# Re-ordering the first batch's chain of an attention-and-MLP kernel: halves of G, pair 1's scores first, and a q wrap read by split matmuls

## The chip, the cores and the metric

The kernel runs on one core of one Trainium2 chip. The metric is the device time of one execution in microseconds, as a median of several executions. The span in a profile is about 1.8 us shorter than that time. Each execution also records the mean clock that was granted to TensorE over the span, 1.0 being full speed.

## The reference

A small attention with 8 batches, 8 heads, 512 local and 32 global positions and head size 64 feeds a two-layer MLP with a hard-swish gate. Local queries see a band of 32 positions each way and all global keys.

```python
k_all = np.concatenate([k_g, k_l], axis=2)
v_all = np.concatenate([v_g, v_l], axis=2)
out_g = np.matmul(sm(scale * np.matmul(q_g, k_all.transpose(0, 1, 3, 2))), v_all)
mask = np.abs(pos[:, None] - pos[None, :]) <= 32
s_ll = np.where(mask, scale * np.matmul(q_l, k_l.transpose(0, 1, 3, 2)), -1e9)
s_l = np.concatenate([scale * np.matmul(q_l, k_g.transpose(0, 1, 3, 2)), s_ll], axis=-1)
out_l = np.matmul(sm(s_l), v_all)
# ... heads side by side -> x of 4352 rows by 512
h = x @ w_in
out = (h * np.clip(h + 3.0, 0.0, 6.0) / 6.0) @ w_out
```

## The kernel before

Two heads of a batch form a "pair", so a batch has four pairs. For batches 0 and 1 TensorE transposes k and q. "G" is the transposed k_g. It is broadcast into free columns of kT (`kglob`), v_g likewise into the shifted V (`vglob`). The scores of a pair come in two chunks: chunk 0 needs only the pair's own k, chunk 1 also needs G. The q of a pair is stored with its last 32 columns repeated in front (the "wrap"), so that every score matmul reads 128 consecutive columns. In batch 0, VectorE copies that wrap out of the q that ScalarE has just written.

```python
def emit_T(p, qdve=False):              # cut: transposes of k and q into PSUM
    nc.vector.tensor_copy(out=kv[...], in_=ps["k"])             # k copy
    qcopy(out=qT[:, W:Sl + W], in_=ps["q"])                     # q copy, ScalarE or VectorE
    if b == 0:
        nc.vector.tensor_copy(out=qT[:, 0:W], in_=qT[:, Sl:Sl + W])   # the wrap
    ...

# opening (cut), every engine in program order
warm_up(17)            # filler matmuls on zeros
...
emit_T(0); emit_Sm(0, 0); emit_Sm(0, 1); emit_Ss(0, 0)   # masks, then pair 0's chunk 0
warm_up(3)
emit_T(1)
emit_G(0, 1, "kg"); kglob(0, nc.vector); vglob(0, nc.vector)
emit_Ss(0, 1)          # pair 0's chunk 1: needs G
emit_S(1, 0)           # pair 1's chunk 0: does not
emit_T(2); emit_S(1, 1); warm_up(2); emit_S(2, 0)
...
```

The softmax here doesn't subtract the row's maximum and nothing guards it: scores larger than these inputs give would overflow.

## Time and profile before

| | before |
|---|---|
| first timed runs | 319.76, 321.0, 321.62, 322.47 us |
| the profiled execution | 319.11 us, span 317.3, clock 0.999 |
| TensorE busy | 305.0 us, 96% of the span |
| TensorE idle from 5 to 50 us | 6.4 us |

The lines that carried the reading are in the prediction below: the page's head, busy time by stretches, what TensorE waits for, and the chain of waits around pair 1.

### The profile page before, as it was taken

To read this page: it belongs to the slowest core of one execution; us is meant where nothing else is said; L and a number is where in the kernel's file an instruction comes from. 1 tells how busy PE (TensorE), PEld (TensorE's weight loads), DVE (VectorE), ACT (ScalarE), POOL (GpSimd) and SP (SyncE) were. 2 spreads that over 40 slices of the span, in tenths; PEclk is the share of its full clock that TensorE was granted. 3 is DMA by queue.
4 is the path that set the end of the run, shared out by engine and by line. 5 is a ranking of instruction groups with operands and counts; after the bars stand their busy time and mean duration, and the time that the engine had idled before them with its cause. 6 is when DMAs were issued, how large, how long until landed. Compare 5 with 4: busy or idle time off the path is not lost.

```text
span 317.3 us, 7316 instructions
## 1 busy us (share of the span) xinstructions
PE 305.0 (96%) x2674; PEld 162.7 (51%) x2674; DVE 214.5 (68%) x486; ACT 199.7 (63%) x416; POOL 152.8 (48%) x273
## 2 busy tenths in 40 slices
PE   8698899999999999999999999999999999999995
PEld 5454564545555455555555555555555554448444
DVE  5578688897755898679955886468934962379101
ACT  6647777887443995479844994589656941589000
POOL 4777998598866654763675456444410000000000
PEclk9999999999999999999999999999999999999999
DMA  7999999999999998799999996999542002100131
GB/s 207 258 301 333 298 310 314 219 192 216 204 222 231 173 204 144 162 202 203 163 156 209 204 188 138 164 213 160 112 115 86 17 19 83 66 2 1 35 99 66
DMA packets 140260, 53.05 MB, mean 167 GB/s; under 512 B 127552, under 2 KB 131904, under 8 KB 140224
## 3 DMA queue, kind: packets, MB, share of 16 engines
q1 hardware_dynamic: 138048, 52.32, 76.2%
q0 software_dynamic: 2176, 0.26, 1.3%
q8 instruction: 21, 0.34, 0.5%
q14 instruction: 15, 0.12, 0.2%
HBM read 35.13 MB, written 8.91 MB: 139 GB/s over the span
## 4 chain that ended last, share of the span: by engine, by line
PE 79%; DVE 12%; ACT 3%; issue 2%; DMA 2%; SPq 0%; POOL 0%
PE po L455 35%; PE psH L439 29%; DVE gt L446 5%; PE psS L268 3%; DVE xn L358 2%; DVE E L275 2%; PE pav L350 2%; PE pav L353 2%; DMA stg<-in_q_l_dram 2%; PE psSG L324 1%; PE psS L293 1%; PE po L467 1%; PE pg L390 1%; PE psS L281 1%; PE psX L411 1%
## 5 line engine op out<-in xcount | busy, mean ns | idle before, releaser
L455 PE MATMUL po<-wout,gt 128*128 128x512 f16 x528 | 122.6, 379 | 0.0
L439 PE MATMUL psH<-xt,win 128*128 128x512 f16 x512 | 119.3, 379 | 1.5 <-DVE gt L446 1.4
L446 DVE SCALAR_TENSOR_TENSOR gt<-t,psH 128x512 f16<-128x512 f32 (+1 forms) x144 | 89.9, 651 | 19.6 <-ACT t L444 18.9
L444 ACT ACTIVATE t<-psH,half_col 128x512 f32<-128x512 f32 (+1 forms) x144 | 92.3, 670 | 14.5 <-PE psH L439 12.9
L439 PEld LDWEIGHTS <-win 128*128 128x128 f16 x576 | 53.3, 98 | 52.6 <-issue 1.6
L455 PEld LDWEIGHTS <-gt 128*128 128x128 f16 x528 | 48.4, 98 | 52.2
L275 DVE TENSOR_TENSOR E<-E,mk 128x512 f16<-128x512 f16 x96 | 51.4, 580 | 30.9 <-ACT E L272 30.2
L272 ACT ACTIVATE E<-psS 128x512 f16<-128x512 f32 x96 | 49.8, 604 | 13.7 <-PE psS L268 13.6
L459 ACT COPY ot<-po 128x512 f32<-128x512 f32 x16 | 9.4, 586 | 58.6 <-PE po L455 53.1
L140 POOL CAST kn<-stg 128x512 f16<-128x512 f32 x31 | 19.0, 614 | 31.8 <-DMA stg<-in_k_l_dram 31.1
L376 POOL TENSOR_TENSOR s<-Eg 128x128 f32<-128x128 f16 x24 | 10.8, 450 | 39.5 <-ACT Eg L325 39.0
L459 DVE COPY ot<-po 128x512 f32<-128x512 f32 x17 | 11.7, 689 | 22.9 <-PE po L455 22.3
L358 DVE TENSOR_TENSOR xn<-pav,rc 128x256 f16<-128x256 f32 x64 | 26.0, 421 | 1.3
L140 POOL CAST qn<-stg 128x512 f16<-128x512 f32 x31 | 19.5, 629 | 11.4 <-DMA stg<-in_q_l_dram 10.4
L140 POOL CAST vt<-stg 128x512 f16<-128x512 f32 x32 | 21.1, 659 | 7.2 <-DMA stg<-in_v_l_dram 6.0
L144 POOL COPY vb<-vt 64x512 f16<-64x512 f16 x32 | 21.4, 669 | 2.1
L302 ACT ACTIVATE E<-psS 128x512 f16<-128x512 f32 x32 | 16.9, 607 | 8.1 <-PE psS L293 8.1
L350 PE MATMUL pav<-vt,E 128*128 128x65 f16 x256 | 19.9, 194 | 0.0
L353 PE MATMUL pav<-vb,E 128*128 128x65 f16 x256 | 19.9, 195 | 0.0
L350 PEld LDWEIGHTS <-E 128*128 128x128 f16 x256 | 17.9, 99 | 3.3
L353 PEld LDWEIGHTS <-E 128*128 128x128 f16 x256 | 16.8, 97 | 3.1
L268 PEld LDWEIGHTS <-kT 64*128 64x128 f16 x384 | 10.8, 94 | 9.8 <-issue 7.9
(92 smaller groups left out, 276.6 us busy)
## 6 DMA issues: line engine op xcount, KB each, us to landing
stg<-in_k_l_dram SPq DMA_DIRECT2D x32, 256.0 KB, 3.6
stg<-in_q_l_dram SPq DMA_DIRECT2D x32, 256.0 KB, 4.0
stg<-in_v_l_dram SPq DMA_DIRECT2D x32, 256.0 KB, 4.6
out_dram<-ot SPq DMA_DIRECT2D x23, 256.0 KB, 3.6
stg<-in_moe_w_in_dram SPq DMA_DIRECT2D x16, 256.0 KB, 5.9
stg<-in_moe_w_out_dram SPq DMA_DIRECT2D x16, 256.0 KB, 4.8
out_dram<-ot SPq DMA_DIRECT2D x8, 192.0 KB, 3.6
out_dram<-ot SPq DMA_DIRECT2D x16, 64.0 KB, 1.8
```

The costliest lines, as they stand in the source:

```text
L140: eng.tensor_copy(out=o, in_=s[c + "f"])
L144: eng.tensor_copy(out=vbs[b % NV][0:D, :, m, vc], in_=vts[b % NV][D:P, :, m, vc])
L272: nc.scalar.activation(out=E[:, ch, e], in_=pss[2 * ch + e], func=EXP, scale=qk_scale)
L275: nc.vector.tensor_tensor(out=E[:, ch, e], in0=E[:, ch, e], in1=mk[:, ch].rearrange("p w c -> p (w c)"), op=mult)
L350: nc.tensor.matmul(out=o, lhsT=E[:, 0, e, w * P:(w + 1) * P], rhs=vt[:, w, m, c], start=True, stop=False, skip_group_check=True)
L353: nc.tensor.matmul(out=o, lhsT=E[:, 1, e, w * P:(w + 1) * P], rhs=vb[:, (w - 1) % NT, m, c], start=False, stop=True, skip_group_check=True)
L358: nc.vector.tensor_tensor(out=xn[:, 2 * w2:2 * w2 + 2].rearrange("p w (e d) -> p w e d", e=2), in0=po[:, :, 1:1 + P].rearrange("p w (e d) ...
L439: nc.tensor.matmul(out=ps[:, 0:n], lhsT=w_in_t[m][:, c * P:(c + 1) * P], rhs=rhs(m), start=(m == 0), stop=(m == NM - 1), skip_group_check= ...
L444: nc.scalar.activation(out=t1[:, 0:n], in_=ps[:, 0:n], func=RELU, bias=half_col, scale=1.0 / 6.0)
L446: nc.vector.scalar_tensor_tensor(out=gts[c][:, 0:n], in0=t1[:, 0:n], scalar=1.0, in1=ps[:, 0:n], op0=amin, op1=mult)
L455: nc.tensor.matmul(out=po[t][:, 0:dm], lhsT=gts[c][:, t * P:(t + 1) * P], rhs=w_out_t[c // 4][:, c % 4], start=(c == 0), stop=(c == NC - 1))
L459: (nc.scalar.copy if t % 2 else nc.vector.tensor_copy)(out=ot, in_=po[t][:, 0:dm])
```

## The change

It shortens the chain at the start, where TensorE waits for small copies on VectorE and ScalarE. G's copies and broadcasts go in halves, so that pair 0's second chunk needs only the first half. Pair 1's first chunk goes ahead of pair 0's second one. The wrap is no longer copied in batch 0: the first block of a score row is computed by two matmuls, 32 columns from the end of q and 96 from its start. Pair 4's transposes move behind the broadcast for batch 1, three copies change engine (pair 2's q to VectorE, pair 3's q and pair 2's x to ScalarE), two fillers go, and two loads are moved.

```diff
+            parts = [(w * P, w * P, P)]
+            if w == 0 and p < NM:
+                parts = [(0, Sl, W), (W, W, P - W)]
+            for o, i, n in parts:
+                for e in range(2):
+                    nc.tensor.matmul(out=pss[e][:, o:o + n], lhsT=kT[r, c0:c0 + P], rhs=qT[r, i:i + n], ...)
 ...
+    load_g(1, 4, "kg")
     load(4, "kq")
-    load_g(1, 4, "kg")
 ...
-    load_vg(1)                       # was among the first loads
 ...
     cast(4, "kq", nc.gpsimd)
+    load_vg(1)
 ...
-    emit_T(1)
-    emit_G(0, 1, "kg")
-    kglob(0, nc.vector)
-    vglob(0, nc.vector)
-    emit_Ss(0, 1)
+    emit_Tp(1); copy_k(1); copy_q(1)           # one per line in the kernel
     emit_S(1, 0)
+    emit_Gp(0, 1, "kg")
+    copy_G(0, 1, "kg", 0); kglob_m(0, lo)
+    emit_S(0, 1)
+    copy_G(0, 1, "kg", 1); kglob_m(0, hi)
 ...
-    warm_up(2)
+    vglob_m(0, lo)
 ...
-    emit_T(4)
     cast_G(1, 4, "kg")
 ...
     kglob(1, nc.vector)
+    emit_T(4)
```

More of the change, by code (lines that the diff above doesn't have):

```diff
@@ L192, in cast_G, with emit_Gp @@
         gst[b0, nm, "n"] = n
-    def emit_G(b0, b1, nm):
+    def emit_Gp(b0, b1, nm):
         nb = b1 - b0
@@ L198, in emit_G @@
         n = gst[b0, nm, "n"]
-        psT = ps_tile("psGT", FP16)
+        psT = gst[b0, nm, "ps"] = ps_tile("psGT", FP16)
         for j in range(nb):
@@ L202, in emit_G, with copy_G, kglob_m, vglob_m @@
                              rhs=ident, is_transpose=True)
-        MH = NM // HH
-        for x in range(HH):
-            kv = psT[x * D:(x + 1) * D, 0:nb * P].rearrange("p (b m e s) -> p e b m s", b=nb, m=MH, e=2)
-            for e in range(2):
-                r, ms = slice(e * D, (e + 1) * D), slice(x * MH, (x + 1) * MH)
-                o = kgT[r, ms, b0:b1] if nm == "kg" else qgz[r, ms, b0:b1, e]
-                nc.vector.tensor_copy(out=o.rearrange("p m b s -> p b m s"), in_=kv[:, e])
+    MH = NM // HH
+    def copy_G(b0, b1, nm, x):
+        nb = b1 - b0
+        kv = (gst[b0, nm, "ps"][x * D:(x + 1) * D, 0:nb * P]
+              .rearrange("p (b m e s) -> p e b m s", b=nb, m=MH, e=2))
+        for e in range(2):
+            r, ms = slice(e * D, (e + 1) * D), slice(x * MH, (x + 1) * MH)
+            o = kgT[r, ms, b0:b1] if nm == "kg" else qgz[r, ms, b0:b1, e]
+            nc.vector.tensor_copy(out=o.rearrange("p m b s -> p b m s"), in_=kv[:, e])
+    def emit_G(b0, b1, nm):
+        emit_Gp(b0, b1, nm)
+        for x in range(HH):
+            copy_G(b0, b1, nm, x)
+    def kglob_m(b, ms):
+        kv = kTs[b % 2][:, ms, 0:NT * KW].rearrange("p m (u c) -> p m u c", u=NT)
+        n = ms.stop - ms.start
+        nc.vector.tensor_copy(out=kv[:, :, :, P:KW],
+                              in_=kgT[:, ms, b].unsqueeze(2).to_broadcast([P, n, NT, Sg]))
+    def vglob_m(b, ms):
+        n = ms.stop - ms.start
+        nc.vector.tensor_copy(
+            out=vbs[b % NV][rg, :, ms, vc],
+            in_=vg[rg, b].rearrange("s (m h) d -> s m (h d)", h=2)[:, ms].unsqueeze(1)
+            .to_broadcast([Sg, NT, n, P]))
     def kglob(b, eng):
@@ L214, in kglob, with emit_Tp, copy_k, copy_q @@
                         in_=kgT[:, :, b].unsqueeze(2).to_broadcast([P, NM, NT, Sg]))
-    def emit_T(p, qdve=False):
+    def emit_Tp(p):
         b, m = divmod(p, NM)
         s = st[p]
-        kT = kTs[b % 2][:, m]
-        kv = kT[:, 0:NT * KW].rearrange("p (u c) -> p u c", u=NT)
-        qT = wrk.tile([P, Sl + W], FP16, tag="qT", name="qT", bufs=5)
-        ps = {}
+        s["kT"] = kTs[b % 2][:, m]
+        s["qT"] = wrk.tile([P, Sl + W], FP16, tag="qT", name="qT", bufs=5)
         for c in "kq":
-            ps[c] = ps_tile("psT" + c, FP16)[:, 0:Sl]
+            s["ps" + c] = ps_tile("psT" + c, FP16)[:, 0:Sl]
             for j in range(NT):
-                nc.tensor.matmul(out=ps[c][:, j * P:(j + 1) * P], lhsT=s[c + "n"][:, j], rhs=ident,
-                                 is_transpose=True)
-        qcopy = nc.vector.tensor_copy if qdve else nc.scalar.copy
+                nc.tensor.matmul(out=s["ps" + c][:, j * P:(j + 1) * P], lhsT=s[c + "n"][:, j],
+                                 rhs=ident, is_transpose=True)
+    def copy_k(p):
+        s = st[p]
+        kv = s["kT"][:, 0:NT * KW].rearrange("p (u c) -> p u c", u=NT)
         nc.vector.tensor_copy(
             out=kv[:, :, 0:P].rearrange("p u (i j) -> p u i j", j=NT),
-            in_=ps["k"].rearrange("p (j u i) -> p u i j", j=NT, u=NT))
-        qcopy(out=qT[:, W:Sl + W].rearrange("p (i j) -> p i j", j=NT),
-              in_=ps["q"].rearrange("p (j i) -> p i j", j=NT))
-        if b == 0:
-            nc.vector.tensor_copy(out=qT[:, 0:W], in_=qT[:, Sl:Sl + W])
-        else:
-            nc.scalar.copy(out=qT[:, 0:W].rearrange("p (i j) -> p i j", j=NT),
-                           in_=ps["q"].rearrange("p (j i) -> p i j", j=NT)[:, P - W // NT:P])
-        s["qT"], s["kT"] = qT, kT
+            in_=s["psk"].rearrange("p (j u i) -> p u i j", j=NT, u=NT))
+    def copy_q(p, dve=False):
+        s = st[p]
+        (nc.vector.tensor_copy if dve else nc.scalar.copy)(
+            out=s["qT"][:, W:Sl + W].rearrange("p (i j) -> p i j", j=NT),
+            in_=s["psq"].rearrange("p (j i) -> p i j", j=NT))
+    def emit_T(p):
+        emit_Tp(p)
+        copy_k(p)
+        copy_q(p)
+        s = st[p]
+        nc.scalar.copy(out=s["qT"][:, 0:W].rearrange("p (i j) -> p i j", j=NT),
+                       in_=s["psq"].rearrange("p (j i) -> p i j", j=NT)[:, P - W // NT:P])
     def emit_TD(p):
@@ L290, in emit_Ss @@
             c0 = w * KW if ch == 0 else ((w - 1) % NT) * KW + D
-            for e in range(2):
-                r = slice(e * D, (e + 1) * D)
-                nc.tensor.matmul(out=pss[e][:, w * P:(w + 1) * P], lhsT=kT[r, c0:c0 + P],
-                                 rhs=qT[r, w * P:(w + 1) * P], start=False, stop=True,
-                                 skip_group_check=True)
+            parts = [(w * P, w * P, P)]
+            if w == 0 and p < NM:
+                parts = [(0, Sl, W), (W, W, P - W)]
+            for o, i, n in parts:
+                for e in range(2):
+                    r = slice(e * D, (e + 1) * D)
+                    nc.tensor.matmul(out=pss[e][:, o:o + n], lhsT=kT[r, c0:c0 + P],
+                                     rhs=qT[r, i:i + n], start=False, stop=True,
+                                     skip_group_check=True)
         if exps:
@@ L398, in emit_den, with emit_X @@
                          rhs=Ess[b].rearrange("p m e s -> p (m e s)"), skip_group_check=True)
-    def emit_X(p):
+    def emit_X(p, act=False):
         b, m = divmod(p, NM)
@@ L414, in emit_X @@
         xts.setdefault(b, []).append(xt)
-        nc.vector.tensor_copy(out=xt, in_=psX[:, 0:Sl])
+        (nc.scalar.copy if act else nc.vector.tensor_copy)(out=xt, in_=psX[:, 0:Sl])
     def emit_XG(b):
@@ L619 @@
     u1 = units.pop(0)
-    emit_T(0)
-    emit_Sm(0, 0)
-    emit_Sm(0, 1)
-    emit_Ss(0, 0)
-    warm_up(3)
-    emit_T(1)
-    emit_G(0, 1, "kg")
-    kglob(0, nc.vector)
-    vglob(0, nc.vector)
-    emit_Ss(0, 1)
-    emit_S(1, 0)
-    emit_T(2)
+    lo, hi = slice(0, NM // 2), slice(NM // 2, NM)
+    HEAD = 3
+    emit_Tp(0)
+    copy_k(0)
+    copy_q(0)
+    emit_S(0, 0)
+    warm_up(3)
+    emit_Tp(1)
+    copy_k(1)
+    copy_q(1)
+    emit_S(1, 0)
+    emit_Gp(0, 1, "kg")
+    copy_G(0, 1, "kg", 0)
+    kglob_m(0, lo)
+    emit_S(0, 1)
+    copy_G(0, 1, "kg", 1)
+    kglob_m(0, hi)
+    emit_Tp(2)
+    copy_k(2)
+    copy_q(2, True)
     emit_S(1, 1)
-    warm_up(2)
+    vglob_m(0, lo)
     emit_S(2, 0)
     emit_AV(0)
-    emit_T(3, True)
+    vglob_m(0, hi)
+    emit_Tp(3)
+    copy_k(3)
+    copy_q(3)
     emit_S(2, 1)
@@ L641 @@
     emit_S(3, 1)
+    emit_AV(2)
     emit_X(1)
-    emit_AV(2)
-    HEAD = 3
+    emit_X(2, True)
+    emit_AV(3)
     for c in range(HEAD):
         u1(c, range(2))
-    emit_X(2)
-    emit_AV(3)
+    emit_X(3)
     for c in range(HEAD):
         u1(c, range(2, 3))
-    emit_X(3)
-    emit_T(4)
     cast_G(1, 4, "kg")
@@ L661 @@
     emit_T(5)
-    vglob(1, nc.vector)
+    vglob_m(1, lo)
+    vglob_m(1, hi)
     u1(5)
```

## The prediction

> **What bounds the kernel now.** I read four views, coarse to fine. First the page's head: which engine fills the span.
>
> ```profile
> span 317.3 us, 7316 instructions
> PE 305.0 (96%) x2674; PEld 162.7 (51%) x2674; DVE 214.5 (68%) x486; ACT 199.7 (63%) x416; POOL 152.8 (48%) x273
> ```
>
> TensorE is the bound over the whole: 12.3 us of 317.3 are not busy. Then the busy time by stretches, to see where those 12.3 us lie (columns: stretch, its length, then busy us of PE, PEld, DVE, ACT, POOL, granted clock, DMA share, GB/s).
>
> ```profile
> 5.00:10.00 5.00, 3.52 (x31) 1.91 (x28) 1.91 (x6) 2.26 (x4) 2.19 (x4) 1.00 1.17 298
> 10.00:15.00 5.00, 3.87 (x56) 2.16 (x57) 2.92 (x8) 3.44 (x8) 4.29 (x7) 1.00 1.13 229
> 25.00:30.00 5.00, 3.69 (x27) 1.51 (x27) 4.76 (x12) 4.31 (x9) 3.59 (x6) 1.00 1.06 323
> 35.00:40.00 5.00, 4.04 (x50) 2.11 (x48) 3.75 (x10) 3.25 (x8) 4.82 (x9) 1.00 1.17 269
> 50.00:60.00 10.00, 10.00 (x95) 5.49 (x93) 7.97 (x14) 7.63 (x18) 5.89 (x11) 1.00 1.15 280
> ```
>
> From 5 to 50 us PE idles 6.4 us (the rows shown hold 1.5, 1.1, 1.3 and 1.0 of it; the others I read gave 0.5, 0.3, 0 and 0.8). The first microsecond is start, 4 us are the last output's way home, and between 50 and 300 us the idle is 1.4. So what a rewrite of the opening can win is capped at about 6.4 us, 2.0% of the span, plus the two removed filler matmuls (0.2 us) and slack inside "busy" while a group waits half way. What PE waits for, up to 60 us:
>
> ```profile
> PE psS L293 <- DVE kT L213: 2.2, 2, 1.2
> PE psGT L201 <- DVE kgn L191: 1.4, 2, 1.0
> PE psS L293 <- DVE kT L229: 0.8, 1, 0.8
> PE psSG L324 <- DVE qgz L209: 0.8, 1, 0.8
> PE psS L293 <- DVE qT L235: 0.5, 1, 0.5
> PE psTq L226 <- POOL qn L140: 0.4, 1, 0.4
> ```
>
> The change aims at rows 1 and 2 (G, its copies and the broadcast into kT), at row 5 (the q wrap) and at some of row 3. Rows 4 and 6 are untouched: row 4 is a DVE chain at 49 us, row 6 hangs on the q load of pair 1, 5.29 us under way. Last, the chain of waits in the first knot:
>
> ```profile
> 8.71 0.59 ACT qT L232
> 9.32 0.17 DVE qT L235
> 9.50 0.14 DVE kgn L191
> 9.68 0.24 PE psGT L201
> ...
> 10.78 0.30 DVE kT L213
> ...
> 11.13 0.40 PE psS L293 x8
> ```
>
> The cut holds four kgT copies (9.95 to 10.75). The wrap of q stands on DVE ahead of the cast of G, though G does not need it: pair 1's q delays G.
>
> **What the Trainium skill says.** "Perfetto Trace Analysis", section Identifying Performance Opportunities: work on the most contended engine, find its gaps and what each waits for; matmul busy share is no measure of the distance to peak. The trace agrees: 96% busy, yet a group's busy time includes waits inside it. "TensorE: Matmul & The Clock Gate", Part 1: the array falls to half clock after an idle window of about 3.4 us, so the two dropped fillers matter only if a gap of that size opens. Here the longest PE wait after the start is 1.2 us, and the four mask matmuls at 5.45 are the last slow ones (1.45 us against 1.03 later); I expect no loss. "SBUF — State Buffer", the reading of its diagram: VectorE's two-port copies and GpSimd exclude each other. The trace fits: one V shift took 0.95 us beside the 0.98 us V broadcast, 0.61 elsewhere. Splitting the broadcast moves that collision, it does not remove it.
>
> **The change, part by part.** The order of instructions of the two programs (compared without running) differs in the first 30-odd us only: DVE has 3 fewer wraps from SBUF and other splits, ACT exchanges one q copy for one xt copy, PE gains 16 score matmuls (8 chunks, each with its first block of 128 columns cut in 32 and 96, two heads) and loses 2 fillers. From the fifth pair's scores on, the streams are the same. So I carried the new order through by hand with the durations of before: exponentials 0.49 us apart, k copy 0.60, q copy 0.59 on ACT and 0.60 on DVE, one head of AV on PE 0.50 and its normalization on DVE 1.11, a transposed group 0.22, a 512-column matmul 0.216.
>
> 1. Pair 0's wrap (0.17 plus a hop): scores at about 6.3 instead of 6.84. Worth nothing by itself, for pair 1's q transposes still wait for the Pool cast, at 8.27.
> 2. Pair 1: q copy ends 9.30; scores go at 9.33, G's transpose at 9.7, two kgT copies (0.38) and half a broadcast (0.2) end at 10.55. Pair 0's second chunk starts there, before it was 11.13: 0.6 us. More on ACT: the exponentials of chunk (1,0) start at 9.8, so the four that ended at 13.63 end near 12.1: 1.5 us. From here ACT sets the pace.
> 3. Pairs 1 to 3: q of pair 2 is copied by DVE, freeing 0.5 us of ACT. The last exponentials end at 18.7, not 20.75: 2.1 us.
> 4. MLP head: AV(3) and the xt copies end at 22.2, not 24.55. The win casts on Pool nearly bind: the second ended at 20.1 and the fourth at 21.4, fed straight by DMA. T(4) goes behind, its q copy off ACT. The last quarter of the head starts at 22.3, not 24.60: 2.3 us.
> 5. Given back: pair 4's k copy (0.60) now stands behind kglob(1) on DVE, on the way to pair 4's scores. Three gates, four kgT copies, one gate, the broadcast and the k copy end at 27.9; the scores of pair 4 end at 28.6, not 30.3: 1.7 us.
> 6. Given back again: ACT did pair 4's exponentials in two lots (29.06 and 30.41, end 31.5); now it does four in a row from 28.3 to 30.4: 1.1 us, plus some 0.3 of idle before pair 5's that goes. Through t, gate, AV(4) and the k copy, pair 6's scores start at 36.75, not 38.13: 1.4 us.
> 7. The floor below this is Pool:
>
> ```profile
> 33.47 0.61 POOL L140 CAST kn<-stg 128x512 f16<-128x512 f32 x1
> 34.02 0.61 POOL L140 CAST qn<-stg 128x512 f16<-128x512 f32 x1
> ```
>
> Pair 6's q cast ends at 34.63, and PE used it at 34.74: 0.1 us of slack. Pool runs unbroken from 27.29, when pair 5's k landed, with DMA at 1.06 to 1.17 in that part. The change moves bytes among the loads but takes none away, and puts a 0.6 us descriptor job (v_g of batch 1) ahead of later casts, probably into a wait for data (0.5 and 0.84 us there). So the transposes of pair 6 cannot come sooner; PE would be there at 32.7 and waits two microseconds. With them done at 34.9, two groups of 0.86 bring the scores of pair 6 to 36.6 at best. That agrees with 36.75 and caps the gain at about 1.5.
>
> After that nothing is re-ordered; the wait at 49 us (0.8) stays and the gain is carried. Sum: 1.4 us, less a little for 16 extra matmuls (8 take 0.33 us, so 16 are at most 0.65, mostly inside waits): 1.3 us. 321.62 − 1.3 = 320.3 us.
>
> **Rivals.** (a) All the idle in the opening goes and is not given back: 2.3 to 4 us, 317.5 to 319.3. For it: step 4 has 2.3 in hand. Against: Pool's casts, and DMA over 1.0. (b) Pool gets later, by the descriptor job or by pair 4's loads standing behind 192 KB of G: 0.6 us more at step 7 leaves 0.7, 320.9. (c) The early removal of the v_g load frees DMA for the first loads (0.5 us of all engines by the share of that queue, 1.3% for 8 loads) and pair 5's k lands sooner: the floor sinks with it, gain 2, 319.6. (d) v_g of batch 1 lands late (5.7 us under way) and blocks DVE before the gates: loses up to 1 us; it would be issued near 24 and wanted near 29.7, so it is close, but the gate behind it waits for ACT until 31.7. (e) Nothing visible: the three timed runs spread over 2.7 us, twice the gain.
>
> **Range and chances.** Centre 320.2, pulled slightly towards (c) and (a), since the author must have seen a gain. 80%: 318.6 to 321.6. Faster by over 2% needs 315.2, the whole cap: 1.5%. Slower by over 2% would need a new stall of 6 us, with no buffer cut and the same streams behind: 1%.
>
> **What would show it.** Right: PE's waits on kT's broadcast (2.2) and on G's cast (1.4) fall to under half; the wait on the wrap (0.5) goes; a new wait of PE's transposes on Pool's kn or qn of 1 to 2 us stands at 32 to 35; idle from 50 us on is as before; the end moves by what the scores of pair 6 move. Wrong: Pool's cast of pair 6 is itself over 1 us earlier (then the gain is larger); or the gain at 37 us is absorbed later, by a growing wait on gt around 100 us or a DMA transpose near 75.

## The result, and the profile after

Before took 321.31 us (319.76 to 322.47, 4 runs), after 317.61 us (317.2 to 318.07, 4 runs). The ratio is 0.9888, with a 95% interval of 0.9843 to 0.9933. Ratios here are the record's, taken over the fast runs of both kernels in the same rounds, so they are not quite the ratio of the medians. All runs count as fast but one: a run of before at 323.28 us in the last round, which is over 1.5% above the fastest one beside it. It is left out below. The measured time lies below my range.

The page's head of the changed kernel, and its busy time by the same stretches (columns as in the prediction):

```profile
span 315.8 us, 7343 instructions
PE 304.3 (96%) x2688; PEld 161.9 (51%) x2688; DVE 213.9 (68%) x484; ACT 200.1 (63%) x417; POOL 152.6 (48%) x273
```

```profile
5.00:10.00 5.00, 2.97 (x39) 1.59 (x37) 1.34 (x3) 2.26 (x4) 1.98 (x4) 1.00 1.15 310
10.00:15.00 5.00, 4.70 (x79) 2.70 (x73) 3.79 (x12) 4.27 (x9) 4.25 (x7) 1.00 1.03 223
...
25.00:30.00 5.00, 3.79 (x39) 1.82 (x37) 4.48 (x11) 3.09 (x8) 3.53 (x6) 1.00 1.15 331
...
35.00:40.00 5.00, 4.27 (x57) 2.61 (x56) 4.06 (x12) 3.51 (x8) 4.28 (x9) 1.00 1.09 285
```

The span fell by 1.5 us only, 317.3 to 315.8, while the median fell by 3.7. So the two profiles explain less than half of the result. From 5 to 10 us TensorE works 0.55 us less, from 10 to 15 us 0.8 us more; at 25 to 30 and 35 to 40 there is little change. What TensorE waits for in the changed kernel, up to 60 us (total us, times, longest):

```profile
PE psS L326 <- DVE kT L252: 1.2, 3, 0.7
PE psTk L246 <- POOL kn L140: 1.1, 1, 1.1
PE psH L472 <- POOL win L174: 1.0, 2, 0.6
...
PE psTq L246 <- POOL qn L140: 0.6, 2, 0.4
...
PE psS L326 <- DVE kT L223: 0.3, 1, 0.3
```

The wait on the broadcast (2.2 us before) is down to 0.3, the ones on G's cast (1.4) and on the wrap (0.5) are gone from the list. In their place stand Pool's casts: pair 1's k, and the weights of the MLP head. The chain of waits around pair 1 (start us, us, what):

```profile
8.72 0.41 PE psTq L246 x4
9.15 0.59 ACT qT L258
9.79 0.41 PE psS L326 x10
10.20 0.18 PE psGT L201
...
10.81 0.24 DVE kT L223
11.10 0.41 PE psS L326 x10
```

The ten-matmul rows are split score groups. The cut holds two kgT copies where before had four. From pair 1's q transposes to pair 0's second chunk it takes 2.38 us, not 2.86, and TensorE now works in between. That is the knot second by second, before and then after:

```profile
8.00:9.00 1.00, 0.40 (x4) 0.23 (x4) 0.62 (x1) 0.65 (x2) 0.48 (x2) 1.00 1.23 306
9.00:10.00 1.00, 0.23 (x1) 0.10 (x1) 0.35 (x3) 0.29 (x1) 0.70 (x2) 1.00 1.14 310
10.00:11.00 1.00, 0.00 (x0) 0.00 (x0) 0.93 (x5) 0.00 (x0) 0.48 (x2) 1.00 1.19 304
11.00:12.00 1.00, 0.87 (x11) 0.34 (x12) 0.97 (x2) 0.44 (x1) 0.94 (x2) 1.00 1.32 245
```

```profile
8.00:9.00 1.00, 0.59 (x9) 0.42 (x10) 0.65 (x2) 0.00 (x0) 0.62 (x1) 1.00 1.19 298
9.00:10.00 1.00, 0.76 (x15) 0.35 (x11) 0.17 (x2) 0.59 (x1) 0.75 (x2) 1.00 1.17 293
10.00:11.00 1.00, 0.79 (x11) 0.19 (x5) 0.55 (x3) 0.78 (x2) 0.49 (x2) 1.00 1.19 293
11.00:12.00 1.00, 0.90 (x19) 0.80 (x20) 0.79 (x5) 0.76 (x2) 0.94 (x2) 1.00 1.27 249
```

TensorE is busy 1.5 us of these four before (the first figure behind the comma), 3.05 after. Matching equal instructions on ScalarE by their start shows how far ahead the changed kernel is: 1.0 us at 48 us, 0.7 at 85, 1.6 from 128 us to the end. The last step, 0.9 us between 103 and 115 us, is not the change's: the second profile of the unchanged kernel (the first run below) is ahead of the first by 0.2 us at 100 us and by 1.1 at 115.

### The profile page after: what moved, and what is told of

It is laid out like the page before. It is cut to its first block, busy times and chain, and to the rows that moved or that the text cites. A ratio compares the mean times of both kernels' runs of the same rounds, so it can differ in the third digit from the quotient of the medians.

```text
span 315.8 us, 7343 instructions
## 1 busy us (share of the span) xinstructions
PE 304.3 (96%) x2688; PEld 161.9 (51%) x2688; DVE 213.9 (68%) x484; ACT 200.1 (63%) x417; POOL 152.6 (48%) x273
## 4 chain that ended last, share of the span: by engine, by line
PE 81%; DVE 8%; ACT 6%; issue 2%; DMA 2%; SPq 0%; POOL 0%
PE po L488 34%; PE psH L472 32%; PE psS L297 3%; DVE gt L479 3%; PE pav L383 2%; PE pav L386 2%; ACT t L477 2%; DVE xn L391 2%; DMA stg<-in_q_l_dram 2%; DVE E L304 2%; PE psSG L357 1%; PE psS L326 1%; ACT E L335 1%; PE po L500 1%; ACT E L301 1%
## 5 line engine op out<-in xcount | busy, mean ns | idle before, releaser
L301 ACT ACTIVATE E<-psS 128x512 f16<-128x512 f32 x96 | 49.9, 605 | 13.5 <-PE psS L297 13.4
L140 POOL CAST kn<-stg 128x512 f16<-128x512 f32 x31 | 19.8, 640 | 34.7 <-DMA stg<-in_k_l_dram 33.1
L140 POOL CAST qn<-stg 128x512 f16<-128x512 f32 x31 | 20.3, 656 | 11.3 <-DMA stg<-in_q_l_dram 11.3
L144 POOL COPY vb<-vt 64x512 f16<-64x512 f16 x32 | 20.2, 631 | 2.1
L335 ACT ACTIVATE E<-psS 128x512 f16<-128x512 f32 x32 | 16.9, 600 | 4.8 <-PE psS L326 4.8
```

The source lines that it names most:

```text
L140: eng.tensor_copy(out=o, in_=s[c + "f"])
L301: nc.scalar.activation(out=E[:, ch, e], in_=pss[2 * ch + e], func=EXP, scale=qk_scale)
```

## The experiments

The question was where the other two microseconds come from. "Full clock" means a mean granted clock of 0.998 or more, "low" one of 0.995 or less; nothing lay between. (The 0.998 in the changed kernel's profile comes from the last microsecond, when its work is done: 0.50 granted there. The start is not in the figure either: the record of the granted clock begins at 4.1 to 6.9 us, and until then 128-column transposes start 107 ns apart, afterwards 56 ns.)

**Repeats, and the two moved loads.** No edit in the first two.

> The kernel before, unchanged, to get a second profile of it and more times. In the first pair of profiles the spans differ by 1.5 us (317.3 and 315.8) but the timed medians by 3.7 (321.31 and 317.61): the profiled execution of before, at 319.11, was faster than all four timed ones. Theory F (the first profile of before was a lucky draw): this profile has a span over 318.5 us, timed runs 319.5 to 322.5, and shows an extra wait of 1 to 3 us that the first did not have. Theory S (the profile is typical, the timed runs were slowed by something from outside): timed runs here near 319.1 and span 317.3, ratio to before 1.000.

> The changed kernel, unchanged, for spread. Both theories: 317.2 to 318.1 us, ratio 0.986 to 0.991 by theory F; by theory S 0.995, as the profiles say (1.5 us).

The third moves the loads in the kernel before, the fourth puts them back in the changed one:

```diff
-    load(4, "kq")
     load_g(1, 4, "kg")
+    load(4, "kq")
 ...
-    load_vg(1)
 ...
     cast(4, "kq", nc.gpsimd)
+    load_vg(1)
```

> Before, with only the two loads moved (k_g of batches 1 to 3 ahead of pair 4's k and q; v_g of batch 1 issued by Pool after pair 4's casts). Rival L (the gain beyond my 1.3 us comes from the early bandwidth that the v_g load no longer takes, so that pair 5's k lands sooner): ratio 0.992 to 0.995. Main theory (the re-sequencing of the compute engines gives the gain): ratio 0.998 to 1.003.

> The changed kernel with the two loads put back where they were. Rival L: ratio to before 0.993 to 0.997, that is 1.5 us or more worse than the changed kernel. Main theory: 0.987 to 0.991, within 0.5 us of the changed kernel; k_g of batches 1 to 3 lands over 1 us later, so its cast may hold the gates of the head up to 1 us.

Before again took 320.08 us (0.9992), after again 317.49 (0.9921), before with the loads moved 320.26 (0.9998), after with the loads undone 318.06 (0.9943). After with the loads undone came out in rival L's range, but by two low runs (319.54 and 321.03 us); its four full-clock runs average 317.57, as the changed kernel's. The loads give no gain by themselves. What gave the answer was the clock of each run of before again:

```
318.21 318.47 318.69   clock 1.0   1.0   1.0
321.48 321.73 321.75   clock 0.995 0.995 0.989
```

The time goes with the clock. The profile that was taken here is again a full-clock one (span 316.7), so theory F's expected span was missed; but the profile of the third kernel (span 318.5, clock 0.995) caught the event. Its busy time, with the granted clock as the third figure from the right:

```profile
12.00:12.25 0.25, 0.25 (x5) 0.12 (x6) 0.25 (x1) 0.25 (x2) 0.25 (x1) 0.98 1.03 164
12.25:14.00 1.75, 1.75 (x18) 1.16 (x14) 0.73 (x2) 1.75 (x5) 1.69 (x4) 0.50 1.09 203
14.00:15.50 1.50, 1.50 (x13) 0.74 (x12) 0.27 (x1) 0.70 (x2) 1.37 (x3) 0.50 0.99 259
15.50:15.75 0.25, 0.25 (x3) 0.04 (x1) 0.00 (x0) 0.25 (x2) 0.25 (x1) 0.70 0.92 246
```

TensorE ran at half clock from about 12.24 to 15.65 us, 3.4 us long, right behind its idle stretch. It is busy all that time and gets half as much done: the 128-column transposes at 12.7 to 13.4 us start 107 ns apart, those at 16.9 to 17.3 us 56 ns. By 18 us this run is 1.85 us behind the first profile of before, at 100 us 2.0, at the end 1.2 (1.8 behind the second profile of before). Half of 3.4 us in a span of 318 is 0.0054, which is a mean clock of 0.995: the number in each run's record counts such windows.

Over all rounds 49 fast executions of before have a recorded clock, besides the one first profiled, and 10 of the changed kernel:

| | runs | mean us |
|---|---|---|
| before, full clock | 9 | 318.69 |
| before, 0.994 or 0.995 | 29 | 320.52 |
| before, 0.993 or less | 11 | 321.75 |
| before, all | 49 | 320.46 |
| after (all at full clock) | 10 | 317.72 |

The change gains 320.46 − 317.72 = 2.7 us. Of that, 318.69 − 317.72 = 1.0 us is there at equal clock, and 320.46 − 318.69 = 1.8 us is the half clock that 40 of 49 runs of before meet and no run of after. (The first medians differed by 3.7 us, from four runs of each; the clocks of those four runs of before are not on record.)

**Is idle TensorE the cause?** Fillers in the two waits of before:

```diff
     emit_T(1)
+    warm_up(7)
     emit_G(0, 1, "kg")
+    warm_up(9)
     kglob(0, nc.vector)
```

> The kernel before, with 7 and 9 more filler matmuls in the two waits of TensorE around pair 1 and G (8.7 to 9.7 us and 9.9 to 11.1 us). [...]Theory C (a window of about 3.4 us in which TensorE is under half busy costs a window of half clock; in before every window that starts between 6.9 and 9.1 us is one, in the changed kernel hardly any): all runs at clock 0.998 or more, median 318.4 to 319.0, ratio to before 0.993 to 0.996, low spread. Rival D (the scatter comes from DMA landings in the opening, the clock only follows): runs at 0.995 remain in about two of three, median 320.2, ratio 1.000.

All six runs at full clock. The fillers took 0.11 us each and left waits of 0.24 and 0.22 us. 319.37 us (0.9952, the interval 0.992 to 0.9983); the before runs beside it had one of eleven at full clock. Work that computes nothing makes the kernel faster, so the idle stretch is the cause and rival D falls. The six average 319.3 us, 0.6 more than before at full clock, though, and over the 318.4 to 319.0 that I expected. In the profile the delay is not in the fillers' stretch (from 8.7 to 29 us ScalarE's starts are equal to 0.03 us) but in one broadcast, which is in the timelines of before, of this run, and of the changed kernel:

```profile
29.36 0.57 DVE L213 COPY kT<-kgT 128x512 f16<-128x512 f16 x1
```

```profile
29.39 1.04 DVE L213 COPY kT<-kgT 128x512 f16<-128x512 f16 x1
```

```profile
27.54 0.29 DVE L235 COPY kT<-kgT 128x512 f16<-128x512 f16 x1
```

The same copy takes 0.29, 0.57 or 1.04 us, and pair 4's scores wait for it. The Trainium skill ("SBUF — State Buffer", the reading of its diagram) says that VectorE's two-port copies and GpSimd take a shared port pair in turn. The traces fit only in part: in the two slow cases a copy of V on GpSimd starts within 0.05 us of this one, but in the second profile of before the copy takes 0.29 us while GpSimd casts. No run takes GpSimd away, so the cause is not shown, and one profile cannot account for the mean of six runs.

**Half the fillers**, 3 and 4 in place of 7 and 9.

> The kernel before with 3 and 4 fillers in the two waits instead of 7 and 9. They add 0.75 us to windows that hold about 0.7 us of work in 3.4: a lowest share of about 0.42 instead of 0.2. If the share in the window decides and the limit lies near 0.4 to 0.5, as the other kernels suggest: one to three of six runs fall to a clock of 0.995 (before: four in five), the others take 318.7 to 319.3. If any activity is enough: none of six. If the fillers must fill: five of six.

Three of six runs low, the other three 318.76 to 319.06. So that something runs in the waits is not enough. Six runs do not tell three of six from before's four in five; the windows below do. In its profile (clock 0.989) pair 1's k came late as well (a wait of 1.4 us on its cast), and the granted clock is 0.50 from 11.0 to 17.8 us, two windows in a row.

To compare kernels, I slid a window of 3.413 us (the length that the skill's "TensorE: Matmul & The Clock Gate", Part 1, gives, and the one seen above) over each profile from 1.5 to 45 us and took the lowest share in which TensorE shows as busy.

| kernel | lowest share | low runs |
|---|---|---|
| before, two profiles | 0.24, 0.20 | 40 of 49 |
| before, loads moved | 0.18 | 5 of 6 |
| before, half fillers | 0.33 | 3 of 6 |
| after, pair order back | 0.37 | 2 of 6 |
| after, pair 4's transposes early | 0.42 | 0 of 6 |
| before, split wrap | 0.46 | 2 of 6 |
| after, two profiles | 0.48, 0.65 | 0 of 10 |
| after, v_g early; G whole | 0.54; 0.54 | 2 of 6; 0 of 6 |
| before, split and fillers; fillers | 0.56; 0.58 | 0 of 6; 0 of 6 |
| after, loads undone; wrap back | 0.62; 0.62 | 2 of 6; 2 of 6 |
| after, no fillers | 0.69 | 0 of 6 |

The order is right on the whole, with exceptions. One profile is one draw of when the loads landed (the changed kernel alone has 0.48 and 0.65), so a kernel may show 0.62 and still have low runs.

The traces say more than this table. In the four profiles that caught a half clock, it begins one or two lengths of 3.413 us after the first entry of the clock record (from 5.41 to 12.24 us in the first one), and it ends one or two lengths later. So the windows lie on a grid that each run starts at its own time, 4.1 to 6.9 us in the 16 profiles. Counted on that grid, these are the windows least busy:

| profile | window, us | TensorE busy | clock granted next |
|---|---|---|---|
| before, loads moved | 8.83 to 12.24 | 35% | 0.50 |
| after, pair order back | 6.48 to 9.90 | 47% | 0.50 |
| before, half fillers | 7.56 to 10.98 | 48% | 0.50 |
| before, split wrap | 8.14 to 11.55 | 52% | 0.50 |
| after, G whole | 26.00 to 29.41 | 55% | 1.00 |
| after, pair 4's transposes early | 4.57 to 7.98 | 56% | 1.00 |
| before again | 6.42 to 9.84 | 58% | 1.00 |
| before | 6.30 to 9.72 | 59% | 1.00 |

Every other window at full clock in the 16 profiles is 57% busy or more, and full clock follows it until the work ends. (At half clock, a window 65% busy was followed by a second one at half clock, in the half-filler profile.) So the limit lies between 52% and 55% here, and the two profiles of before kept the full clock by where their grid fell. In them, windows that start within 2.6 and 3.0 us are under 53.5% busy; of 3.4 us that is 77% and 87%, an estimate of the runs that are hit if the grid falls anywhere; 82% were.

**Are the changed kernel's own fillers needed?** `warm_up(3)` taken out.

> The changed kernel without its three filler matmuls at 6.3 us. Theory C: windows that start between 5.3 and 6.7 us fall to a busy share of 0.33 to 0.5, so one to three of six runs show a clock of 0.995 and take 319.5 to 320.5 us; the others stay at 317.5. Rival D: nothing changes, 317.5 throughout.

317.62 us, 316.98 to 317.7, no run low. My expectation was a miss: with pair 1's scores ahead of G the stretch is filled by work.

**The split alone, and the rest without the split.** In the first, the split matmuls of the diff above go into before and the wrap copy out. In the second, the changed kernel gets this:

```diff
+        if p < NM:
+            nc.vector.tensor_copy(out=s["qT"][:, 0:W], in_=s["qT"][:, Sl:Sl + W])
 ...
-            if w == 0 and p < NM:
-                parts = [(0, Sl, W), (W, W, P - W)]
```

> The kernel before with the q wrap read by split score matmuls and nothing else changed. G's cast no longer stands behind pair 1's wrap: it goes at about 8.7 instead of 9.4, so pair 0's second chunk starts at 10.4 instead of 11.1. By my prediction's step 2: at full clock 0.4 to 0.8 us better than before (317.9 to 318.3). Theory C: the low windows start from 6.9 to about 8.5 instead of 9.1, so the half clock still comes in about half of the runs; median 318.2 to 320.

> The changed kernel with the wrap copied by VectorE as before and the score matmuls whole. If the re-ordering and not the split gives the gain at full clock: 317.5 to 317.9. If the split carries it: 318.2 to 318.6. Theory C: the wrap delays pair 1's first scores by 0.2 us and no more, so no run falls under clock 0.998.

The split alone: 318.76 us, 0.9926 (0.9897 to 0.9954), full-clock runs 318.31 on average against 318.69, two of six low. The low ones, 318.67 and 318.92 us, are no slower than the slowest full-clock one, 318.93: one half window does not cost 1.8 us in every kernel. The re-ordering without the split: 319.62 us, 0.9967, full-clock runs 319.47, two of six low; I expected 318.2 to 318.6 and no low run. At full clock that is worse than before by 0.8 us. Its waits show why:

```profile
PE psS L326 <- DVE qT L262: 2.2, 4, 0.7
PE psS L326 <- DVE kT L252: 1.7, 2, 0.9
PE psGT L201 <- DVE kgn L191: 1.4, 2, 1.3
```

In the new order all four pairs wait for the wrap on VectorE. The re-ordering needs the split.

**Single parts of the order.** Pair 4's transposes put back ahead of G's cast (`emit_T(4)` moved up); only the v_g load put back; pair 1's first chunk put back behind pair 0's second (`emit_S(1, 0)` moved down); G and its broadcasts whole again, ahead of pair 0's second chunk.

> The changed kernel with pair 4's transposes and copies put back ahead of G's cast for batches 1 to 3. My prediction's step 5 says that the new place gives back 0.6 us (the k copy behind the broadcast, on the way to pair 4's scores). If so: 316.9 to 317.2, 0.4 to 0.6 us better than the changed kernel (317.5). The rival says that the old place makes the transposes wait for Pool's cast of pair 4 and holds VectorE's cast of G and the ACT's first t by the q copy: 317.5 to 318.2.

> The changed kernel with only the v_g load of batch 1 put back to the start. In the changed kernel its 0.6 us of descriptor work stands ahead of the casts of win that hold the MLP head (1.0 us of TensorE's wait). Without it the head should be 0.3 to 0.6 us earlier at 35 us; at the end 317.0 to 317.4. Rival: the load then competes with pair 1's k and q at the start and nothing is won: 317.5 to 318, perhaps with one run of six at clock 0.995.

> The changed kernel with pair 1's first scores put back behind pair 0's second chunk. By my step 2, at full clock 0.5 to 1.0 us worse than the changed kernel (318.0 to 318.5), for the exponentials start at 10.9 and not at 10.2. Theory C: TensorE is then idle from 9.1 to 10.6 but for G's transpose, windows that start near 6.5 to 7.5 us fall under half busy, and one to three of six runs show a clock of 0.995 and cost 1.5 to 2 us more. Rival: order does not matter, 317.5.

> The changed kernel with G, its broadcast into kT and the one of V whole, ahead of pair 0's second chunk, as before. Two kgT copies and half a broadcast more (0.65 us) on the way to that chunk, and 1.0 us of V broadcast on VectorE ahead of pair 2's k copy: by my working 0.4 to 0.8 us worse than the changed kernel (317.9 to 318.3). Rival: ACT, busy with pair 1's exponentials until 11.3, hides it: 317.5.

| | median us | ratio to before | full-clock mean | low |
|---|---|---|---|---|
| pair 4's transposes early | 318.18 | 0.9938 | 318.11 | 0 of 6 |
| v_g early | 319.02 | 0.996 | 318.59 | 2 of 6 |
| pair order back | 318.7 | 0.9965 | 318.24 | 2 of 6 |
| G whole | 318.48 | 0.9946 | 318.34 | 0 of 6 |
| changed kernel, 10 runs | 317.52 | 0.9921 (a2) | 317.72 | 0 of 10 |

With any one of these four undone, the full-clock mean is 0.4 to 0.9 us higher. The full-clock runs of one kernel scatter by some 1 us and the changed kernel did not run in these rounds, so I rank none of the four, and the 0.4 of pair 4's transposes is not clear of the scatter. Pair order and G whole came out as expected (0.5 to 1.0 and 0.4 to 0.8); the low runs with the pair order back are the clock again, with 0.50 granted from 10 to 13.25 us in its profile. Pair 4's early transposes and the early v_g load were misses: I expected a gain from each. With the early transposes VectorE's gates of the head start at 24.94 us and not at 24.05, behind the k copy and the cast of G, and the broadcast starts at 28.43, not 27.54: the k copy holds one thing or the other, as the second half of the rival said.

**The smallest version.** Before with the split matmuls and 3 and 9 fillers around G, nothing else:

```diff
     emit_T(1)
+    warm_up(3)
     emit_G(0, 1, "kg")
+    warm_up(9)
```

> The kernel before with the q wrap read by split score matmuls, and 3 and 9 fillers in the waits that are left around G. If the split and the clock are all that the change is worth: no run under clock 0.998, median 317.5 to 317.9, as the changed kernel. If the re-ordering gives something of its own at full clock: 318.2 to 318.6 (the split alone had 318.3 at full clock), with no run under 0.998.

317.79 us (317.31 to 317.85), 0.9904 (0.9871 to 0.9938), all at full clock. It equals the changed kernel (its runs average 317.70, the changed kernel's 317.72). So the split and a busy TensorE are enough for the whole gain, by the first outcome. Why it is 0.6 us ahead of the split alone at full clock (317.70 against 318.31) is not shown; it may be scatter. The re-ordering is one way to keep TensorE busy; fillers are another. No version beat the changed kernel: the one without fillers, 317.62, is not distinguishable from it.

## Why the prediction was wrong

- **The step that failed** is the sentence on the clock: "the array falls to half clock after an idle window of about 3.4 us, so the two dropped fillers matter only if a gap of that size opens. Here the longest PE wait after the start is 1.2 us [...] I expect no loss." I asked only whether the change could lose the clock, never whether before was already losing it. This term stood at zero in the sum and measured 1.8 us. It needs no gap of 3.4 us: three waits of 0.4, 1.0 and 1.2 us in a row, with little between, leave a window 20 to 24% busy; the window that the third kernel's profile caught was 35% busy.
- **The base was one profile.** It was a full-clock one, at 319.11 us, below every timed run. I subtracted a gain read from that profile from a median of runs that mostly had the half clock. Rival (e) took the scatter for noise; it was the mechanism.
- **The sum of the steps** was 1.3 us and measured 1.0 at equal clock: right in kind, a little large. Step 2 was right in its chain: 2.38 us against 2.28 worked out, though it began at 8.72 and not at 8.27 us, for pair 1's q was under way for 5.72 us and not 5.29. Steps 3 to 6 arrived late: the last exponentials ended at 19.6 (18.7 predicted), the scores of pair 4 at 29.0 (28.6), and those of pair 6 began at 37.14 (36.75). Step 3 saw pair 2's q copy leave ScalarE and missed that pair 3's comes back to it: in the traces both kernels make six of the large q copies on ScalarE and one on VectorE. (The wraps that go are four, not three.)
- **Step 1** called pair 0's wrap worthless. That holds for pair 0. But I put no value on the wraps of all four pairs together. Without the split the re-ordering is 319.47 at full clock, with it 317.72: 1.75 us.
- **Step 5** is wrong as a give-back: the old place of pair 4's transposes is no better (318.11).
- **Step 7**, Pool as the floor, was half right. Pool's q cast of pair 6 ended at 34.22 and its transposes began at 34.28, with 0.16 us of wait, not two: TensorE itself came later. The win casts held it for 1.0 us, of which rival (b) had the direction. Its descriptor job is not the reason: with that job moved away (v_g early) the wait is still 0.9 us. Two of those casts waited on GpSimd for their DMA, 0.44 and 0.34 us.
- **Rival (c)**, the early v_g load, is not settled. Putting it back alone cost 0.9 us at full clock, putting both loads back cost nothing (317.57), and each had two low runs of six. Whether an early v_g load brings the half clock by delaying pair 1's k and q stays open, as do the steps of up to 1 us between 76 and 130 us that differ from run to run.

## What to carry to other kernels

Look at the granted clock of every timed run, not of the profiled one alone. A mean of 0.995 over 318 us is one window of half speed. It cost the kernel before nearly 2 us, and if the profile happens to be a full-clock run, none of its lines shows it. Where TensorE waits several times in a few microseconds, cheap filler matmuls that fit in the waits can win back what the half clock costs. When several changes come together, put each into the old kernel and take each out of the new one: here the re-ordering without the split is worse than nothing at equal clock.

## What the Trainium skill lacked or had wrong

- "TensorE: Matmul & The Clock Gate", Part 1: its table gives an idle window of about 3.4 us as the way back to half clock. Here windows that were 35 to 52% busy did it in four profiles, and no wait of TensorE in these was over 1.5 us; 45 of 55 fast runs of before, and of before with the loads moved, had it. Its section "A second HAM failure mode: psum-queue depth-cycling" says that frequent micro-idles can make the clock oscillate; I passed over it. What it lacks is a number for how much idling: on the grid above, 52% busy or less was followed by half clock, 55% or more was not.
- The same page says that the window is 3413 ns long and runs free. The trace agrees: 0.50 granted from 12.24 to 15.65 us, in some runs of one kernel and not in others. What it lacks is how to find the windows of a run: they count from the first entry of the clock record, 5.41 us in that trace.
- "Perfetto Trace Analysis", Identifying Performance Opportunities, has no word on the granted clock. Its advice to find the gaps on the most contended engine found the gaps, but not the 1.8 us that they cost behind them.
- "SBUF — State Buffer" on the shared ports has no size for a small copy. The same 128x512 copy took 0.29, 0.57 and 1.04 us in three profiles.
